# Tiles at multiples of 512 bytes, and a warm-up with fp32r matmuls of ones

## The chip, the cores and the metric

The kernel runs on one core of one Trainium2 chip. The metric is the device time of one execution in microseconds (us); lower is better. The engines are named as in the profile: PE (TensorE, the matmul engine) with PEld for its weight loads, DVE (VectorE), ACT (ScalarE), POOL (GpSimd) and SP (SyncE, which issues most of the transfers). A pair below is two matmuls, one on partitions 0 to 63 and one on partitions 64 to 127, that the array works on side by side.

## What is computed

The reference is a lightweight causal convolution followed by two feed-forward layers without residuals, on 16,384 tokens of width 192:

```python
# x [4, 4096, 192], weight [8, 7]: a softmax over the 7 taps of each of 8 heads,
# then a causal convolution over the sequence with those taps
w = softmax(weight, axis=-1)
out[b, s, h, g] = sum_k w[h, k] * x_pad[b, s + k, h, g]
x = out.reshape(16384, 192)
h = x @ w_in;               x = (h * cos(h)) @ w_out        # layer 1, 192 -> 2048 -> 192
h = max(x @ w_in2, 0);      out = (h * h) @ w_out2          # layer 2, 192 -> 2048 -> 192
```

## The kernel before

Activations lie transposed: features on partitions, tokens along the free dimension, in 32 blocks of T = 512 tokens. The 2048 hidden features are 16 chunks of 128. Every fp32 factor is split into a high and a low part of type fp32r (tiles `xs` for the activations, `g` for the hidden values, `wt1`, `wt2`, `wt3` for the weights), and a product is the sum of three fp32r matmuls (of two in part of the output products).

All matmuls of the two layers have 64 rows: `half` (line 528) takes 64 of the 128 partitions of a weight slice `w[k, o : o + P]` (128 columns) and of a moving tile of 512 columns. `Group.write` issues them alternately for the lower and the upper 64 partitions, so that they run in pairs. `first_products` makes groups for h (input products, line 528 in the profile as `h<-xs,wt`), `second_products` for the output (`o<-g,wt`).

DVE and ACT carry the work between the two products: per chunk of layer 1 a cosine (lines 729, 741, 748, 755) and the split of g (781, 786); per chunk of layer 2 a relu, a square and the same split. They also split the weights: lines 289 to 360, chunk pair by chunk pair, during the first part of the run. DVE makes the convolution of most blocks tap by tap (line 409).

The convolution of the first four blocks (`ON_PE = 4`) is done on PE: six groups of seven pairs of plain fp32 matmuls, with a diagonal matrix of each tap as the weights (`diag`, in the tile `early`) and a shifted block as the moving operand (`x[:, k : k + T]`, line 528 in the profile as `h<-early`). A plain fp32 matmul leaves two MATMUL records in the trace, an fp32r matmul one. ACT (482) and DVE (486) split the results into `xs`.

Ahead of all that stands the warm-up (line 1121): `WARM = 6` pairs of fp32 matmuls of a broadcast constant, `quarter`, into two accumulation banks `o`; nobody reads their result. POOL sets the constants and makes the identity `ident` (lines 174, 175, 446 to 457), from which DVE and ACT make the diagonals once the softmax on DVE (lines 194 to 226) has given `wtap`.

The order of the instructions is planned while the program is built: `Order.run` simulates the engines with fixed costs (`PAIR = 233` ns for a pair) and puts each engine's steps into one fixed order; at run time an engine waits for semaphores in that order. The change leaves these costs alone. Tiles of the pool `const` are laid out in SBUF one behind the other, in the order in which `const.tile` is called.

Of the kernel before, what the change touches and what calls it, by code (L numbers as in the profile page):

```python
# [8 lines left out]
F32 = mybir.dt.float32  # L9
# [9 lines left out]
PAD = K - 1  # L19
DFF = 2048  # L20
NT = B * S
P = 128
R = D - P
T = 512
NB = NT // T
NC = DFF // P
LEAD = 6
WARM = 6
ON_PE = 4
LATE = 4  # L30
EARLY = 4
LAGS = (3, 2)
BUFS = {"raw": 2, "s": 2, "m": 2, "x": 4, "t": 11, "g": 12, "h": 4, "o": 4, "xs": 4}


# [18 lines left out]
def f32(t):  # L54
    return t.bitcast(F32)
# [97 lines left out]
def tile_kernel(  # L153
# [8 lines left out]
    nc = tc.nc  # L162
    V, A, G = nc.vector, nc.scalar, nc.gpsimd
    order = Order()

    const = ctx.enter_context(tc.tile_pool(name="const", bufs=1))
    psum = ctx.enter_context(tc.tile_pool(name="psum", bufs=1, space=PSUM))

    def tiles(kind, shape, dtype, pool=const):
        order.free[kind] = [(0.0, i, pool.tile(shape, dtype, name=f"{kind}{i}")) for i in range(BUFS[kind])]  # L170

# [69 lines left out]
    OA_H, OA_L = (HI + R + P, HI + R + 3 * P), (LO + P, LO + 3 * P)  # L241
    X_H, X_L = HI + R + 4 * P, LO + 4 * P
    OX = (0, HI + U - R)
    wts = [const.tile([P, NC // 2 - n, WC], F32R, name=f"wt{l}") for l, n in ((1, 0), (2, LATE))]

    shared = ctx.enter_context(tc.tile_pool(name="shared", bufs=1))
# [119 lines left out]

    spread_at = {(0, 1): (0, 0, 0), (2, 3): (3, 4, 4)}
    first_slot = {n: at[1 + k] for ab, at in spread_at.items() for k, n in enumerate(ab)}
    tiles("x", [P, T + PAD], F32)
    tiles("t", [P, T], F32)  # L370
    tiles("g", [P, T], F32R)
    tiles("h", [P, T], F32, psum)
    tiles("o", [P, T], F32, psum)
    parts = [[const.tile([P, T], F32R, name=f"xs{i}{j}") for j in range(4)] for i in range(BUFS["xs"])]
    order.free["xs"] = [(0.0, i, p) for i, p in enumerate(parts)]
    def cast(e):
        return A.copy if e == "A" else V.tensor_copy

# [2 lines left out]
    def conv(n, due):  # L381
# [5 lines left out]
        for j in (0, 1):  # L387
# [35 lines left out]
            def high(s, e, y=y, j=j):  # L423
                cast(e)(own.got["xs"][0][2 * j], y.got["t"][0])  # L424
# [15 lines left out]
    for i in range(2 * ON_PE):  # L440
        at = 2 * K * P + i * (T + PAD)
# [2 lines left out]


    G.memset(ident[:, 0], 1.0)
    G.affine_select(
        out=ident[:, 0],
        in_=ident[:, 0],
# [80 lines left out]
    class Item:  # L530
# [15 lines left out]
        def second(self, bank):  # L546
# [3 lines left out]
            acc = self.acc.got["o"][bank]  # L550
            todo = ((OA_L[odd], gh), (OA_H[odd], gh), (OA_H[odd], gl)) if bank == 0 else ((OX[odd], gh), (OX[odd], gl))
            return [(acc, w, o, x) for o, x in todo]
# [112 lines left out]
    def slot(ins):  # L665
# [5 lines left out]
        for k in (0, 1):  # L671
            lag = LAGS[k] if ins or not ending else 0
            if pend[k] and pend[k][0].slot + lag <= s:
                due[k].append(pend[k].pop(0))
                while pend[k] and pend[k][0].slot + LAGS[k] < s:
                    due[k].append(pend[k].pop(0))
# [168 lines left out]
    def ends(it, done):  # L845
# [60 lines left out]
        if l == 0:  # L906
# [11 lines left out]
            def to(j):  # L918
                return own.got["xs"][0][j]

            xh = order.add(
                "xh" + name, high, lambda s, e: cast(e)(to(0), at(ac)), (ac, own), due=due - 3500
            )
            xl = order.add(
# [14 lines left out]
            )  # L939
            yh = order.add(  # L940
                "yh" + name, high, lambda s, e: cast(e)(to(2), at(bc)), (ys, own), due=due - 1500
            )
            yl = order.add(
# [173 lines left out]

    for i in range(WARM):
        for k, rows in enumerate((lower, upper)):
            bank = order.free["o"][k][2]  # L1120
            nc.tensor.matmul(  # L1121
                bank,
                quarter[rows].to_broadcast([R, P]),
                quarter[rows].to_broadcast([R, T]),
                start=i == 0,
                stop=i == WARM - 1,
            )

    with tc.manual_schedule():
        order.run()  # L1130
# [41 lines left out]
```

## Time and profile before

| | |
|---|---|
| time, median of 3 runs | 2333.3 us (2332.58 to 2333.54) |
| profiled execution, span from first to last instruction | 2330.9 us |
| PE busy | 2322.2 us (100% of the span), 19,696 matmul records |
| DVE busy | 1848.8 us (79%) |
| ACT busy | 1936.2 us (83%) |
| POOL busy | 1.4 us |

The profiled execution's span is 2.4 us under the median of the runs: what lies around the first and the last instruction. [...]

### The profile page before, as it was taken

Reading aid. Unit: us, or ns where it says so; the run is one execution under the profiler, and the core shown is the slowest. Engines: PE = TensorE matmul, PEld = TensorE weight load, DVE = VectorE, ACT = ScalarE, POOL = GpSimd, SP = SyncE. Lnnn points to the kernel's source line nnn. Section 1 sums busy time; section 2 is a strip of 40 time slices with the busy share of each in tenths; the row PEclk is TensorE's granted clock in tenths of the full one; section 3 lists DMA queues with packets and bytes.
Section 4 is the critical chain, followed back from the end, with each engine's and each line's share of the span. In section 5 each row is a group of like instructions: output and inputs, shape, how many; then the busy total and the mean of one; then the engine's idle time right before and its main releaser. Section 6 shows DMA issues by size and latency. Waiting matters only on the chain.

```text
span 2330.9 us, 47119 instructions
## 1 busy us (share of the span) xinstructions
PE 2322.2 (100%) x19696; PEld 2262.9 (97%) x19696; DVE 1848.8 (79%) x2963; ACT 1936.2 (83%) x3284; POOL 1.4 (0%) x10
## 2 busy tenths in 40 slices
PE   9999999999999999999999999999999999999998
PEld 5989999999999999999999999999999999999998
DVE  9988988887778887778877788877788877888642
ACT  5888888888888888888888888888888888888886
POOL 0000000000000000000000000000000000000000
PEclk9999999999999999999999999999999999999999
DMA  4120000000000000000000000000000000000000
GB/s 145 42 78 28 6 1 17 17 17 17 1 17 17 17 17 15 3 17 17 17 17 6 13 17 17 17 17 1 17 17 17 17 17 1 17 17 8 8 8 14
DMA packets 30053, 45.17 MB, mean 19 GB/s; under 512 B 3216, under 2 KB 11408, under 8 KB 29840
## 3 DMA queue, kind: packets, MB, share of 16 engines
q1 hardware_dynamic: 29264, 41.10, 5.8%
q8 instruction: 154, 2.52, 0.4%
q10 hardware_dynamic: 576, 1.06, 0.1%
q14 instruction: 59, 0.48, 0.1%
HBM read 29.56 MB, written 12.58 MB: 18 GB/s over the span
## 4 chain that ended last, share of the span: by engine, by line
PE 99%; DVE 0%; ACT 0%; issue 0%; DVEq 0%; POOL 0%; POOLq 0%
PE o L528 51%; PE h L528 47%; PE o L1121 0%; ACT t L765 0%; DVE s L330 0%; DVE g L786 0%; ACT t L774 0%; DVE xs L486 0%; DVE m L307 0%; DVE s L289 0%; DVE m L321 0%; DVE wt L356 0%; ACT s L297 0%; ACT wt L351 0%; DVE t L860 0%
## 5 line engine op out<-in xcount | busy, mean ns | idle before, releaser
L528 PE MATMUL o<-g,wt 64*128 64x512 f32 x10240 | 1432.3, 392 | 1.2 <-DVE g L786 0.4
L528 PE MATMUL h<-xs,wt 64*128 64x512 f32 x9216 | 1312.3, 392 | 0.5
L528 PEld LDWEIGHTS o<-g,wt 64*128 64x128 f32 x10240 | 1186.4, 185 | 25.3 <-PE o L528 5.9
L528 PEld LDWEIGHTS h<-xs,wt 64*128 64x128 f32 x9216 | 1089.0, 185 | 11.9 <-PE h L528 2.9
L786 DVE TENSOR_TENSOR g<-t,g 128x512 fp32r<-128x512 f32 x1024 | 667.4, 686 | 144.4 <-ACT g L781 138.1
L781 ACT CAST g<-t 128x512 fp32r<-128x512 f32 x1024 | 595.5, 617 | 45.7 <-DVE t L755 30.9
L729 ACT ACTIVATE t<-h,quarter 128x512 int32<-128x512 f32 x512 | 350.3, 689 | 203.2 <-PE h L528 197.4
L755 DVE TENSOR_TENSOR t<-t,h 128x512 f32<-128x512 f32 x512 | 348.1, 684 | 168.3 <-ACT t L748 164.4
L741 DVE TENSOR_TENSOR t<-h,t 128x512 f32<-128x512 f32 x512 | 350.8, 689 | 121.1 <-ACT t L729 113.0
L748 ACT ACTIVATE t<-t,right 128x512 f32<-128x512 f32 x512 | 365.1, 718 | 74.2 <-DVE t L741 74.1
L774 ACT ACTIVATE t<-t 128x512 f32<-128x512 f32 x512 | 317.5, 623 | 5.0
L765 ACT ACTIVATE t<-h 128x512 f32<-128x512 f32 x512 | 299.3, 591 | 22.4 <-PE h L528 22.3
L409 DVE SCALAR_TENSOR_TENSOR t<-x,wtap,t 128x512 f32<-128x512 f32 x336 | 250.7, 746 | 3.8
L879 DVE TENSOR_SCALAR t<-o 128x512 f32<-128x512 f32 x60 | 40.8, 680 | 1.4 <-PE o L528 1.4
L428 DVE TENSOR_TENSOR xs<-t,xs 128x512 fp32r<-128x512 f32 x56 | 38.8, 692 | 1.8
L858 ACT ACTIVATE t<-o 128x512 f32<-128x512 f32 x61 | 36.5, 599 | 1.9 <-PE o L528 0.2
L528 PE MATMUL h<-early 64*128 64x512 f32 x168 | 37.7, 594 | 0.2
L528 PEld LDWEIGHTS h<-early 64*128 64x128 f32 x168 | 17.4, 186 | 19.5 <-issue 13.8
L935 DVE TENSOR_TENSOR t<-t,t 128x512 f32<-128x512 f32 x30 | 20.8, 693 | 14.0 <-ACT t L911 13.9
L406 DVE TENSOR_SCALAR t<-x,wtap 128x512 f32<-128x512 f32 x56 | 26.8, 479 | 0.0
L424 DVE CAST xs<-t 128x512 fp32r<-128x512 f32 x56 | 23.3, 416 | 0.0
L946 DVE TENSOR_TENSOR xs<-t,xs 128x512 fp32r<-128x512 f32 x30 | 20.7, 691 | 1.0
(66 smaller groups left out, 285.5 us busy)
## 6 DMA issues: line engine op xcount, KB each, us to landing
x<-in_xp_dram SPq DMA_DIRECT2D x56, 259.0 KB, 3.0
raw<-in_w_dram SPq DMA_DIRECT2D x16, 512.0 KB, 4.0
out_dram<-t SPq DMA_DIRECT2D x32, 256.0 KB, 2.0
out_dram<-t SPq DMA_DIRECT2D x32, 128.0 KB, 2.2
raw<-in_w_dram SPq DMA_DIRECT2D x16, 128.0 KB, 4.2
raw<-in_w_dram SPq DMA_DIRECT2D x32, 64.0 KB, 3.7
early<-in_xp_dram ACTq DMA_DIRECT2D x4, 259.0 KB, 4.8
early<-in_xp_dram SPq DMA_DIRECT2D x4, 259.0 KB, 3.6
```

What stands on the lines that cost most here:

```text
L409: V.scalar_tensor_tensor(out=t, in0=xk, scalar=wk, in1=t, op0=ALU.mult, op1=ALU.add)
L428: V.tensor_tensor(out=lo, in0=y.got["t"][0], in1=f32(h), op=ALU.subtract)
L528: return nc.tensor.matmul(bank, w[k, o : o + P], x[k], start=st, stop=sp)
L729: lambda s, e: A.activation(s.got["t"][0].bitcast(I32), h(), AF.Identity, bias=quarter),
L741: lambda s, e: V.tensor_tensor(out=t(), in0=h(), in1=t().bitcast(I32), op=ALU.subtract),
L748: lambda s, e: A.activation(t(), t(), AF.Sin, scale=2.0 * math.pi, bias=right),
L755: lambda s, e: V.tensor_tensor(out=s.got["t"][0], in0=t(), in1=h(), op=ALU.mult),
L765: lambda s, e: A.activation(s.got["t"][0], h(), AF.Relu),
L774: lambda s, e: A.activation(a.got["t"][0], a.got["t"][0], AF.Square),
L781: "hi" + i, {"A": 620}, lambda s, e: A.copy(s.got["g"][0], d.got["t"][0]), (d,), (("g", 2),), due=late - 1500
L786: lambda s, e: V.tensor_tensor(out=it.hi.got["g"][1], in0=d.got["t"][0], in1=f32(it.hi.got["g"][0]), op=ALU.subtract),
L879: V.tensor_scalar(s.got["t"][0], b(), sc, None, op0=ALU.mult)
```

## The change

It does two things.

First, it moves tiles in SBUF. A tile `gap` of 56 fp32 words (224 bytes) that nobody uses is put ahead of the weights, and the four `x` tiles, whose rows are 2,072 bytes long, are allocated behind `t`, `g` and `xs` instead of ahead of them. The start of each tile in its partition, modulo 512 bytes, in the built programs:

| tiles | before | after |
|---|---|---|
| `wt1`, `wt2` (weights) | 288 | 0 |
| `g`, `xs` (moving operands), `t` | 416 | 0 |
| `raw`, `s`, `m` (weight preparation) | 288 | 0 |
| `early`, later `wt3` (last four chunk pairs of layer 2) | 224 | 448 |
| `x` (convolution inputs) | 288, 320, 352, 384 | 0, 32, 64, 96 |

All slices of the weights begin at multiples of 512 bytes from the start of their tile, and every moving operand of an fp32r matmul begins at the start of its tile. So these operands lie at multiples of 512 after the change, those in `wt3` at 448 modulo 512.

Second, the last three of the six warm-up pairs go. In their place come 43 fp32r matmuls (line 1146 of the new kernel) that multiply a tile of ones, `g0`, by itself: as pairs of 64 rows (`HALVES`) or as single matmuls of 128 rows (`WHOLE`), over 512, 256 or 480 columns, the last from column 8 on. POOL fills that tile with ones, behind the memset of `ident`.

```diff
-WARM = 6
+WARM = 3
+HALVES, WHOLE = (slice(0, R), slice(R, P)), (slice(0, P),)
+RUNS = (
+    (HALVES, 0, T, 5),
+    (WHOLE, 0, T, 7),
+    (HALVES, 0, T, 2),
+    (WHOLE, 0, T, 4),
+    (HALVES, 0, T, 2),
+    (WHOLE, 0, T // 2, 6),
+    (HALVES, 8, 480, 4),
+)
+GAP = 56
...
+    const.tile([P, GAP], F32, name="gap")
     wts = [const.tile([P, NC // 2 - n, WC], F32R, name=f"wt{l}") for l, n in ((1, 0), (2, LATE))]
...
-    tiles("x", [P, T + PAD], F32)
     tiles("t", [P, T], F32)
...
     order.free["xs"] = [(0.0, i, p) for i, p in enumerate(parts)]
+    tiles("x", [P, T + PAD], F32)
...
     G.memset(ident[:, 0], 1.0)
+    ones = order.free["g"][0][2]
+    G.memset(f32(ones), 1.0)
...
+    for spans, at, n, times in RUNS:
+        for i in range(times):
+            for k, rows in enumerate(spans):
+                bank = order.free["o"][k][2]
+                nc.tensor.matmul(
+                    bank[:, 0:n], ones[rows, 0:P], ones[rows, at : at + n], start=i == 0, stop=i == times - 1
+                )
```

PE before, the end of the warm-up and the first products of the convolution (`early` holds the diagonals and the shifted blocks; the brackets name the engines and queues that an instruction waits for):

```order
L1121 MATMUL o_111<-quarter 128x512
L1121 MATMUL o_112<-quarter 128x512
L528 MATMUL h_107<-early 128x512 [waits DMAHW0_49,DVE_49]
L528 MATMUL h_108<-early 128x512 [waits DMAHW4_49,Activation_49]
L528 MATMUL h_107<-early 128x512 [waits Activation_49]
```

PE now, first where the fp32 pairs of the warm-up give way to the matmuls of ones (`g_92` is the tile of ones):

```order
L1135 MATMUL o_108<-quarter 128x512
L1135 MATMUL o_109<-quarter 128x512
L1146 MATMUL o_108<-g_92 128x512 [waits Pool_49]
L1146 MATMUL o_109<-g_92 128x512
L1146 MATMUL o_108<-g_92 128x512
L1146 MATMUL o_109<-g_92 128x512
```

and at the end of the warm-up, where the same convolution products follow:

```order
L1146 MATMUL o_108<-g_92 128x256 x6
L1146 MATMUL o_108<-g_92 128x480
L1146 MATMUL o_109<-g_92 128x480
L1146 MATMUL o_108<-g_92 128x480
L1146 MATMUL o_109<-g_92 128x480
L1146 MATMUL o_108<-g_92 128x480
L1146 MATMUL o_109<-g_92 128x480
L1146 MATMUL o_108<-g_92 128x480
L1146 MATMUL o_109<-g_92 128x480
L542 MATMUL h_104<-early 128x512 [waits DMAHW0_49,DVE_49]
L542 MATMUL h_105<-early 128x512 [waits DMAHW4_49,Activation_49]
```

Six fp32 matmuls have gone and 43 fp32r matmuls stand in their place, the first of them with a wait for POOL. Behind them PE's instructions stand in the order they had.

POOL before, from its first constants on:

```order
L174 MEMSET quarter 128x1
L175 MEMSET right 128x1
L446 MEMSET ident 128x128
L447 ISA
L447 AFFINE_SELECT ident<-ident 128x128
L457 TENSOR_TENSOR ident<-ident 128x64 x2
```

POOL now, at the same place:

```order
L185 MEMSET quarter 128x1
L186 MEMSET right 128x1
L458 MEMSET ident 128x128
L460 MEMSET g_92 128x512
L461 ISA
L461 AFFINE_SELECT ident<-ident 128x128 [waits Pool_49]
L471 TENSOR_TENSOR ident<-ident 128x64 [waits Pool_49]
```

One memset of 512 columns has come ahead of the making of the identity. On DVE, ACT and SP no instruction is added, removed or moved.

## Rows read from the trace of the kernel before

**Rows 1.** The page: span, busy time by engine, granted PE clock, chain that ended last.

```profile
span 2330.9 us, 47119 instructions
...
PE 2322.2 (100%) x19696; PEld 2262.9 (97%) x19696; DVE 1848.8 (79%) x2963; ACT 1936.2 (83%) x3284; POOL 1.4 (0%) x10
...
PEclk9999999999999999999999999999999999999999
...
PE 99%; DVE 0%; ACT 0%; issue 0%; DVEq 0%; POOL 0%; POOLq 0%
```

**Rows 2.** PE by line and shape: count | busy us, mean ns of a record.

```profile
L528 PE MATMUL o<-g,wt 64*128 64x512 f32 x10240 | 1432.3, 392 | 1.2 <-DVE g L786 0.4
L528 PE MATMUL h<-xs,wt 64*128 64x512 f32 x9216 | 1312.3, 392 | 0.5
...
L528 PE MATMUL o<-quarter 64*128 64x256 f32 x16 | 1.9, 376 | 0.0
```

**Rows 3.** Timeline of PE mid-run: start us, us from first start to last end, count.

```profile
1001.51 1.39 PE L528 MATMUL o<-g,wt 64*128 64x512 f32 x10
1002.68 0.91 PE L528 MATMUL h<-xs,wt 64*128 64x512 f32 x6
1003.38 1.38 PE L528 MATMUL o<-g,wt 64*128 64x512 f32 x10
1004.53 1.62 PE L528 MATMUL h<-xs,wt 64*128 64x512 f32 x12
...
1007.78 1.38 PE L528 MATMUL o<-g,wt 64*128 64x512 f32 x10
```

**Rows 4.** Timeline of PE from 2300 us on.

```profile
2312.05 1.46 PE L528 MATMUL o<-g,wt 64*128 64x512 f32 x10
...
2316.49 8.45 PE L528 MATMUL o<-g,wt 64*128 64x512 f32 x70
```

**Rows 5.** Stretches: busy us (count) of PE, PEld, DVE, ACT, POOL; then granted clock.

```profile
600.00:1000.00 400.00, 400.00 (x3442) 397.27 (x3441) 318.47 (x505) 337.77 (x573) 0.00 (x0) 1.00 0.04 14
...
2306.00:2322.00 16.00, 16.00 (x141) 15.80 (x139) 5.17 (x8) 10.11 (x20) 0.00 (x0) 1.00 0.00 1
```

**Rows 6.** Timeline of PE in the first 45 us.

```profile
7.74 19.09 PE L528 MATMUL h<-early 64*128 64x512 f32 x84
26.26 5.67 PE L528 MATMUL h<-xs,wt 64*128 64x512 f32 x36
31.77 1.90 PE L528 MATMUL o<-quarter 64*128 64x256 f32 x16
```

**Rows 7.** Timeline of PEld, the warm-up: a pair of records each.

```profile
4.59 0.19 PEld L1121 LDWEIGHTS o<-quarter 64*128 64x128 f32 x2 [0.24 <-issue]
5.02 0.19 PEld L1121 LDWEIGHTS o<-quarter 64*128 64x128 f32 x2 [0.24 <-issue]
...
7.74 1.25 PEld L528 LDWEIGHTS h<-early 64*128 64x128 f32 x8 [0.81 <-DVE early L469]
```

**Rows 8.** Timeline of PEld in the convolution products.

```profile
21.08 0.19 PEld L528 LDWEIGHTS h<-early 64*128 64x128 f32 x2 [0.24 <-issue]
21.52 0.19 PEld L528 LDWEIGHTS h<-early 64*128 64x128 f32 x2 [0.24 <-issue]
```

**Rows 9.** Timeline of PE behind a wait: one pair alone, then two pairs.

```profile
33.74 0.50 PE L528 MATMUL h<-xs,wt 64*128 64x512 f32 x2
...
33.74 0.73 PE L528 MATMUL h<-xs,wt 64*128 64x512 f32 x4
```

**Rows 10.** Timelines of POOL, ACT and DVE near the start.

```profile
0.86 0.20 POOL L446 MEMSET ident<- 128x128 f32 x1
...
15.34 0.59 ACT L482 CAST xs<-h 128x512 fp32r<-128x512 f32 x1 [1.07 <-PE h L528]
...
15.44 0.95 DVE L330 SCALAR_TENSOR_TENSOR s<-raw,s 128x768 int32<-128x768 int32 x1
16.31 0.68 DVE L486 TENSOR_TENSOR xs<-h,xs 128x512 fp32r<-128x512 f32 x1
```

**Rows 11.** The chain that ended last, first 60 us: start us, us, what.

```profile
7.76 6.37 PE h L528 x28
...
53.31 0.59 ACT xs L482
...
54.66 0.04 DVE wt L356
```

## Prediction

> **What bounds the kernel now.** [...] The pace comes from starts in the timeline, not from record lengths, which overlap. From 1003.38 to 1007.78 us PE starts 10 + 12 + 10 + 6 = 38 matmuls, of which the last two rows have the same sizes as the two ahead of them [rows 3]: 19 pairs in 4.40 us, 232 ns a pair. There are (10,240 + 9,216) / 2 = 9,728 such pairs [rows 2], 2257 us or 97% of the span. The rest is the warm-up, the convolution on PE and short waits. One nanosecond on a pair is thus worth 9.7 us; one microsecond at the start is worth one microsecond, if it is not taken back.
>
> A measurement of this kernel can tell about 0.2%, 4.7 us, from no change: "same" below means 2328.6 to 2338.0 us.
>
> **The change, part by part: the tiles.** The order on DVE, ACT and SP is untouched, and PE's is untouched behind the warm-up, so nothing of the 97% changes except the addresses. The question is whether 232 ns contains a price for operands at 416 (moving) and 288 or 224 (weights) modulo 512. There is something to explain. A pair of fp32 matmul records of 256 columns takes (1.90 - 0.376) / 7 = 0.218 us [rows 2, 6], and a pair of fp32 records of 512 columns 0.43 us, twice that [rows 8]. An fp32r pair of 512 columns needs 14 ns more than the first. Three readings:
>
> - Other engines disturb PE's reads. No: near the end, with DVE busy for 5.2 of 16 us instead of 318 of 400 [rows 5], 38 matmuls take 4.44 us from 2312.05 to 2316.49 [rows 4] (the rows between repeat the pattern of rows 3), 234 ns a pair.
> - The addresses cost it. Against that stand the convolution products: their blocks start at steps of 4 bytes, one per tap, their weights at 224 modulo 512, and yet each pair of records comes 0.43 us behind the last, the same as the warm-up's with its broadcast constant [rows 7, 8]. So at the fp32 pace no address costs anything. It could still cost at the fp32r pace, which takes columns almost twice as fast; no row has an fp32r matmul at another address.
> - It belongs to the fp32r form at any address. Nothing speaks against this.
>
> I take zero for the tiles, since the only rows with many different addresses show no difference; the bounds are zero and 14 ns a pair. For a loss I see no row: before, all moving operands already had one common remainder modulo 512.
>
> [...]
>
> **The warm-up.** Its last three pairs leave six pairs of records of 0.43 us, the first at 5.02 us [rows 7]; they end near 7.6, and the convolution starts at 7.74, when the first diagonal is there. PE executes in order, so the matmuls of ones start at 5.02 and the convolution waits for them. Their length:
>
> - 9 pairs of halves of 512 columns: 9 x 0.232 = 2.09 us.
> - 4 pairs of 480 columns: 4 x 0.232 x 480 / 512 = 0.87 us.
> - 11 whole matmuls of 512 columns. No row has one. Bounds: 0.218 us, the fastest pair of records over as many array cycles (2.40 in all), and 0.73 - 0.39 = 0.34 us, the step from a first pair to a second behind a wait [rows 9], if none of them overlaps with its neighbour (3.74). I take 0.232, since a pair of halves occupies the whole array just as one whole matmul does: 2.55 us.
> - 6 whole ones of 256 columns: half of that, 0.116 us, 0.70 in all; bounds 0.65 and 6 x (0.116 + 0.108) = 1.34, with the same 0.108 us (0.34 - 0.232) on each.
>
> The sum is 6.21 us, bounds 6.01 and 8.04. The warm-up ends at 11.23 us (11.03 to 13.06), and the convolution starts 3.5 us later (3.3 to 5.3).
>
> The wait for POOL costs nothing: the memset of 128 columns is a 0.20 us record at 0.86 [rows 10], four times as many columns are an estimated 0.8 us, and PE asks for the ones at 5.02. Their delay to the identity is hidden too: the diagonals are needed only at 11.2 now.
>
> How much is taken back? Almost nothing. The convolution's 84 records run without a break to 26.26, where the first layer follows at once [rows 6]. DVE works in order too, and its first instruction that needs PE, line 486 at 16.31, follows line 330 without a pause [rows 10]; its operand is there at 15.34 + 0.59 = 15.93, so it has 0.38 us to spare. Where the chain leaves PE for ACT and DVE at 53.31 [rows 11], DVE's queue decides, and DVE is late by the delay less that 0.38. Net: 3.1 us (2.9 to 5.3; the upper end without the 0.38). Later waits hang on semaphores of these same engines, none on a fixed time, so they move along.
>
> Against the profiled execution: 2330.9 + 3.1 = 2334.0 span. The 2.4 us between span and median stay: 2333.3 + 3.1 = **2336.4 us**, 0.13% more.
>
> **The rivals.**
>
> 1. The addresses did cost the 14 ns (faster). For it: the excess exists, it is independent of the other engines, and the fp32r pace is the one that asks most of the reads. Against it: the convolution products. Time: 2336.4 - 9,728 x 0.0144 = 2196 us; ACT's busy share would go from 84% [rows 5] to 90%, which may give some waits back, so 2196 to 2215. Part of the 14 ns gives anything between; from 0.8 ns a pair on it would count as faster.
> [...]
>
> 2. The whole matmuls don't overlap (slower). They follow one another into one accumulation bank with all 128 rows, where before two halves alternated. If each of the 17 pays 0.34 or 0.224 us, the warm-up ends at 13.06 and the kernel takes 2338.2 to 2338.6. It decides from a warm-up sum of about 7.8 us, that is from some 0.33 us for a whole matmul of 512 columns. For it: fresh starts do cost 0.108 us [rows 9]. Against it: a sequence without waits has shown no such step anywhere. Taking whole record lengths, 0.39 and 0.376 us, gives 9.5 us for the sum and 2340.
>
> 3. The change doesn't do all it says: the last four chunk pairs of layer 2 lie at 448. This would cut rival 1 by a quarter of layer 2's pairs, an eighth of all, to about 2214; it changes nothing for the forecast.
>
> **How the numbers follow.** Forecast, no effect of the addresses and a later start: 0.64. Rivals 1 and 3 in full or in part: 0.19. Rival 2, or another loss at the start or from the new addresses: 0.17. The forecast's own range is 2335.8 to 2338, with 1 us for the spread of the runs 2334.8 to 2338. The range reaches up to 2342 (rival 2 with whole records, and the spread of runs) and down to 2328, a gain of about 1 ns a pair; the larger gains, under 0.2, are left out. Faster 0.19, same 0.64, slower 0.17.
>
> **What would show it.** Right: mid-run, 38 matmuls still take 4.40 us; the first convolution product starts near 11.2 us; line 486 starts about 3.1 us later than 16.31; the whole matmuls of ones come every 0.23 us. Rival 1 shows as fewer than 4.3 us for 38 matmuls, and already in the ones: their first pairs of halves, at 0 modulo 512, would be closer together per column than the pairs from column 8 on. Rival 2 shows as steps of 0.3 us or more between whole matmuls. The prediction is wrong if the pace mid-run differs by 0.5 ns a pair, or if the delay at 7.74 us is not found again at 26 us.

## The result

The changed kernel takes 2293.98 us (median of 4 runs, 2293.3 to 2294.37) beside 2333.42 us for the kernel before on the same chip, 0.9831 times the time, 95% interval 0.9817 to 0.9844. It is 39 us faster, where 3 us slower was forecast and a gain of up to some 5 us was allowed for.

The page of the changed kernel (parts 1, 2 and 4) answers to [rows 1]:

```profile
span 2291.6 us, 47182 instructions
...
PE 2282.5 (100%) x19727; PEld 1988.1 (87%) x19727; DVE 1842.1 (80%) x2963; ACT 1934.0 (84%) x3284; POOL 1.8 (0%) x11
...
PEclk9999999999999999999999999999999999999999
...
PE 99%; DVE 1%; ACT 0%; issue 0%; DVEq 0%; POOL 0%; POOLq 0%
```

PE still holds the chain, at the same granted clock, and the counts on DVE and ACT are the same. What moved is the pace. In stretches of 800 us mid-run (columns: busy us and count of PE, PEld, DVE, ACT, POOL; then clock, DMA share, GB/s), the kernel before and the changed one:

```profile
1400.00:2200.00 800.00, 800.00 (x6882) 794.61 (x6880) 641.80 (x1017) 676.32 (x1146) 0.00 (x0) 1.00 0.04 14
```

```profile
1400.00:2200.00 800.00, 800.00 (x7024) 704.70 (x7022) 643.83 (x1023) 687.80 (x1166) 0.00 (x0) 1.00 0.05 14
```

Some three records of each count only reach over the edge. So 800 / (6879 / 2) = 232.6 ns a pair before, and 800 / (7021 / 2) = 227.9 now. 4.7 ns on 9,728 pairs is 46 us; the span fell by 39.3.

Most of the missing 7 us is at the start. The weight loads of the changed kernel's warm-up show it (start us, us, count; the matmuls start with them or at most one step later):

```profile
4.81 0.19 PEld L1146 LDWEIGHTS o<-g 64*128 64x128 f32 x2 [0.24 <-issue]
5.24 0.89 PEld L1146 LDWEIGHTS o<-g 64*128 64x128 f32 x8 [0.24 <-issue]
6.49 1.46 PEld L1146 LDWEIGHTS o<-g 128*128 128x128 f32 x7 [0.36 <-issue]
8.30 0.30 PEld L1146 LDWEIGHTS o<-g 64*128 64x128 f32 x4 [0.35 <-issue]
8.96 0.76 PEld L1146 LDWEIGHTS o<-g 128*128 128x128 f32 x4 [0.36 <-issue]
10.09 0.30 PEld L1146 LDWEIGHTS o<-g 64*128 64x128 f32 x4 [0.36 <-issue]
10.75 1.64 PEld L1146 LDWEIGHTS o<-g 128*128 128x128 f32 x14 [0.36 <-issue]
```

The seven whole matmuls last from 6.49 to 8.30, the next two pairs to 8.96, the four whole ones to 10.09: 1.81, 0.66 and 1.13 us, each 0.2 us more than 0.23 us a piece (a pair counted as one piece). The convolution follows at 12.63 us (timeline of PE), 4.9 us later than in [rows 6]:

```profile
4.84 7.96 PE L1146 MATMUL o<-g 64*128 64x512 f32 x43
12.63 18.92 PE L542 MATMUL h<-early 64*128 64x512 f32 x84
30.99 5.49 PE L542 MATMUL h<-xs,wt 64*128 64x512 f32 x36
```

### The profile page after: what moved, and what is told of

Same layout as the page of the kernel before. It is cut to its first block, busy times and chain, and to the rows that moved or that the text cites. A ratio compares the mean times of both kernels' runs of the same rounds, so it can differ in the third digit from the quotient of the medians.

```text
span 2291.6 us, 47182 instructions
## 1 busy us (share of the span) xinstructions
PE 2282.5 (100%) x19727; PEld 1988.1 (87%) x19727; DVE 1842.1 (80%) x2963; ACT 1934.0 (84%) x3284; POOL 1.8 (0%) x11
## 4 chain that ended last, share of the span: by engine, by line
PE 99%; DVE 1%; ACT 0%; issue 0%; DVEq 0%; POOL 0%; POOLq 0%
PE o L542 51%; PE h L542 47%; PE o L1146 0%; PE o L1135 0%; ACT t L779 0%; DVE s L342 0%; DVE g L800 0%; ACT t L788 0%; DVE t L769 0%; DVE xs L500 0%; DVE m L319 0%; DVE s L301 0%; DVE m L333 0%; DVE wt L368 0%; ACT s L309 0%
## 5 line engine op out<-in xcount | busy, mean ns | idle before, releaser
L542 PE MATMUL o<-g,wt 64*128 64x512 f32 x10240 | 1362.7, 388 | 1.3 <-DVE g L800 0.5
L542 PE MATMUL h<-xs,wt 64*128 64x512 f32 x9216 | 1244.6, 388 | 0.5
L542 PEld LDWEIGHTS o<-g,wt 64*128 64x128 f32 x10240 | 1035.8, 184 | 142.9 <-PE o L542 5.9
L542 PEld LDWEIGHTS h<-xs,wt 64*128 64x128 f32 x9216 | 935.5, 184 | 128.2 <-PE h L542 2.9
```

The source lines that it names most:

```text
L542: return nc.tensor.matmul(bank, w[k, o : o + P], x[k], start=st, stop=sp)
```

## The experiments

"Difference" below is the remainder modulo 256 of (start of the moving operand minus start of the weights in their partition), in bytes.

### The two halves of the change, each alone

The new addresses without the new warm-up (`e1_align_only`):

```diff
-WARM = 3
+WARM = 6
...
-    ones = order.free["g"][0][2]
-    G.memset(f32(ones), 1.0)
...
-    for spans, at, n, times in RUNS:
-        ...
```

> The new addresses alone, with the old warm-up of six fp32 pairs. In the trace of the changed kernel the first convolution product starts at 12.63 us instead of 7.74, 4.9 us later, of which DVE takes back 0.38. If the addresses give the whole gain and the warm-up only costs: 2294.0 - 4.5 = 2289.5 us (2288 to 2291), mid-run pace 228 ns a pair. If the matmuls of ones had part in the gain: above 2294. If the pace came from something other than addresses: 2333.

Measured: 2289.17 us, 0.9811 (0.9797 to 0.9826). The first branch: the addresses give all the gain, 43.9 us of it.

The new warm-up with the old addresses (`e8_runs_only`), as an edit against the changed kernel:

```diff
-    const.tile([P, GAP], F32, name="gap")
...
+    tiles("x", [P, T + PAD], F32)
     tiles("t", [P, T], F32)
...
-    tiles("x", [P, T + PAD], F32)
```

> The old addresses with the new warm-up (three fp32 pairs, then the 43 matmuls of ones). In the trace of the changed kernel the convolution starts 4.9 us later; less the 0.38 us that DVE has to spare: 2333.1 + 4.5 = 2337.6 us (2336.5 to 2338.5). If PE's delay were taken back later by waits: 2333 to 2335.

Measured: 2338.04 us beside 2333.07, 1.0021 (1.0011 to 1.003): 5.0 us lost, as expected. The two halves add up: 4.8 us lie between the changed kernel and e1. Little of the delay comes back: in the traces the changed kernel is 4.80 us behind e1 at the first convolution product, 4.46 us behind some 45 us later and 4.70 us at the last matmul.

How late the convolution starts also differs between executions. In the profiled one of e8 it starts at 13.76 us, 6.0 us later than before, and the weight loads of the warm-up still come 0.85 us apart beyond 5 us, where in the kernel before they come 0.43 us apart from 4.16 us on:

```profile
3.68 0.34 PEld L1133 LDWEIGHTS o<-quarter 64*128 64x128 f32 x2 [0.51 <-issue]
4.53 0.34 PEld L1133 LDWEIGHTS o<-quarter 64*128 64x128 f32 x2 [0.51 <-issue]
5.38 0.34 PEld L1144 LDWEIGHTS o<-g 64*128 64x128 f32 x2 [0.51 <-issue]
```

The first clock record of the trace, 1.00, stands at 6.50 us in e8, at 3.77 us in the kernel before and at 4.22 us in the changed kernel. A slice of the page is some 58 us long and doesn't show that. So a start that is read from one profile can be a microsecond off, here 6.0 us later beside 4.9.

### Which operand

Moving operands at 0, weights left at 288 (`e2_moving_only`: no `gap` ahead of the weights, the same 224 bytes ahead of `t`), and weights at 0 with the moving operands at 32 (`e3_weights_only`: one `x` tile back ahead of `t`). Edits against e1:

```diff
-    const.tile([P, GAP], F32, name="gap")
...
+    const.tile([P, GAP], F32, name="gap")
     tiles("t", [P, T], F32)
```

```diff
+    x0 = const.tile([P, T + PAD], F32, name="x0")
     tiles("t", [P, T], F32)
...
-    tiles("x", [P, T + PAD], F32)
+    order.free["x"] = [(0.0, 0, x0)] + [(0.0, i, const.tile([P, T + PAD], F32, name=f"x{i}")) for i in (1, 2, 3)]
```

> Old warm-up; moving operands at 0 modulo 512, weights wt1 and wt2 left at 288 (wt3 at 448). Theory M (the moving operand's address costs the 4 to 5 ns a pair): about 2290 us and 228 ns a pair, as with both. Theory W (the weights' address costs it): about 2333 us and 232 ns in layer 1. Theory B (each has its share): in between, 2300 to 2322.

> Old warm-up; weights wt1 and wt2 at 0 modulo 512, wt3 at 448, moving operands at 32 (before 416, both 32 modulo 64). Theory W: about 2290 us, 228 ns a pair. Theory M: about 2333 us, 232 ns. Theory B: 2300 to 2322, and the savings of this kernel and of moving-only add up to those of both, 44 us.

Measured: 2330.74 us (0.9991, 0.9981 to 1.0) and 2339.78 us (1.0028, 1.0017 to 1.004). No theory foresaw this: aligning the moving operands alone gives 2.4 us and aligning the weights alone nothing, where both together give 43.9; aligned weights beside operands 32 bytes off even make the kernel 6.7 us slower than before. In the same stretch of 800 us, e2, then e3:

```profile
1400.00:2200.00 800.00, 800.00 (x6888) 783.65 (x6886) 642.39 (x1019) 676.64 (x1147) 0.00 (x0) 1.00 0.04 14
```

```profile
1400.00:2200.00 800.00, 800.00 (x6861) 794.87 (x6859) 640.39 (x1015) 673.36 (x1141) 0.00 (x0) 1.00 0.04 13
```

By the same working 232.4 and 233.3 ns a pair.

### The last tile

In the change `wt3` lies at 448, 64 bytes short of a multiple of 512. `e4_align_all` brings it to 0, with a filler and with the identity built in a tile of the weight preparation:

```diff
     tiles("x", [P, T + PAD], F32)
+    const.tile([P, 144], F32, name="gap3")
...
-    ident = const.tile([P, 2, P], F32, name="ident")
+    ident = f32(order.free["m"][1][2][:, 0 : 2 * P]).rearrange("p (j c) -> p j c", j=2)
```

> Old warm-up; all of the changed kernel's addresses, and wt3 (last four chunk pairs of layer 2) at 0 instead of 448; the identity is built in a tile of the weight preparation to make room. In the changed kernel matmuls on wt3 follow one another at 229 ns on average instead of 227.5 on wt1 and wt2. If 64 bytes short of a multiple of 512 costs the weights 1.5 ns: 9728 / 4 / 2... a quarter of layer 2's and so an eighth to a quarter of all pairs, 1200 to 2400 x 1.5 ns = 2 to 4 us under the align-only kernel, 2286 to 2288. If the difference is chance: the same as align-only within 1 us.

Measured: 2277.66 us, 0.9763 (0.9748 to 0.9777), 11.5 us under e1, where 2 to 4 were expected. This version beats both kernels. Its stretch:

```profile
1400.00:2200.00 800.00, 800.00 (x7060) 685.03 (x7058) 638.86 (x1015) 690.54 (x1171) 0.00 (x0) 1.00 0.04 13
```

800 / (7057 / 2) = 226.7 ns. The expectation had the share of `wt3` wrong. It holds four of layer 2's eight chunk pairs, so half of that layer's matmuls and a quarter of all. And mid-run nearly every pair is one matmul of layer 1 and one of layer 2 (`first_products` and `second_products` take one item of each list), so one on `wt3` stands in half of all pairs. With the program's order of matmuls laid over the starts of e1's trace (300 to 2250 us), pairs of `wt1` and `wt2` come 227.1 ns apart on average and pairs of `wt1` and `wt3` 228.8; in e4 it is 226.7 and 226.8. 2.0 ns on half of the 9,728 pairs and 0.4 on the other half make 11.7 us.

### Alignment, or the same remainder

The align-all kernel with all tiles behind the gap moved by 32 and by 64 bytes (`e5_shift32`, `e6_shift64`: `GAP = 64` and `GAP = 72`), and with 256 bytes between weights and moving operands (`e10_diff256`: a filler of 64 words ahead of `t`).

> The align-all kernel (2277.7 us) with everything behind the gap moved by 32 bytes: weights, wt3 and moving operands all at 32 modulo 512. The moving-only kernel (0 and 288) and the weights-only kernel (32 and 0) gained nothing, so two theories are left. Theory R (what counts is that weights and moving operands have the same remainder): 2277.7 us, 226.8 ns a pair, as unshifted. Theory A (both must lie at a multiple of some power of two by themselves): 2330 to 2340 us, 232 ns or more.

> The same with 64 bytes: all at 64 modulo 512. Theory R: 2277.7 us. Theory A with 64 as the power of two: 2277.7 us too. Theory A with 128 or more: slower; wt3 at 448 (64 modulo 128) with moving operands at 0 takes 229.2 ns in the align-only kernel, so 2300 us or above.

> The align-all kernel (2277.7 us) with the moving operands at 256 modulo 512, weights and wt3 at 0. Theory P: the difference counts modulo 256, so 2278 us and 226.8 ns a pair. If the period is 512: about 2330 us.

Measured: 2278.34 (0.9766, 0.9752 to 0.9781), 2278.79 (0.9768, 0.9754 to 0.9783) and 2279.7 us (0.9771, 0.9754 to 0.9787). Theory A falls: the multiple of 512 is not what counts. Theory R stands, with one addition from e10: remainders that differ by 256 count as the same (227.0 ns a pair mid-run, by the working above, beside 226.7). With everything at 32, where nothing lies at a multiple of 64, the pace is the same:

```profile
1400.00:2200.00 800.00, 800.00 (x7058) 670.71 (x7056) 639.10 (x1014) 690.27 (x1170) 0.00 (x0) 1.00 0.04 13
```

### The pace at each difference

Two kernels put runs of 24 pairs of ones at chosen addresses in place of the change's 43 matmuls (`e7_probe`, `e9_probe2`; the ones lie in `wt2`, and the diff shows e7's loop). Their times, 2394.78 and 2433.63 us of one run each, hold the longer warm-up and are not of interest.

```diff
+    for spans, w_at, m_at in PROBE:
+        w, m = 1024 + w_at // 4, m_at // 4
+        for n, times in ((T, TIMES), (T // 2, 1)):
+            for i in range(times):
+                for k, rows in enumerate(spans):
+                    bank = order.free["o"][k][2]
+                    nc.tensor.matmul(
+                        bank[:, 0:n], ones[rows, w : w + P], ones[rows, m : m + n], start=i == 0, stop=i == times - 1
+                    )
```

> The changed kernel, with its 43 matmuls of ones replaced by 19 runs of 24 fp32r matmul pairs of 512 columns each (the last two runs: single matmuls of 128 rows), weights and moving operand at chosen remainders modulo 512, a matmul of 256 columns behind each run as a mark. The warm-up gets about 100 us longer; the pace within a run is what is read. Theory R: 227 ns where both remainders agree, (0, 0), (32, 32), (64, 64), and 230 to 235 elsewhere. Theory A: 227 ns only where both are multiples of 64 or 128. If the pace of ones in one place doesn't depend on the address, the loss needs the changing weights and operands of the real products.

> Runs of 24 fp32r pairs of ones as in the first probe, read by the pace within a run. First 20 runs: weights at 0, moving operand at every 16 bytes from 0 to 240, then at 4, 8, 252 and 0. Theory P (the pace depends on moving minus weights modulo 256, as the first probe's 19 runs suggest): 226.7 ns at 0, 229 at 64, 233 at 32, 128, 192 and 224, and values between or above at the steps that have no row yet; whether any difference beats 226.7 is open. Last 6 runs: weights or moving operand replaced by a broadcast of one word. Theory C (the weight load's reads and the moving operand's reads meet in SBUF): with the weights broadcast the pace no longer depends on the address, about 218 to 227 at 0, 32 and 128; the same with the moving operand broadcast. If only one of the two matters, the other broadcast leaves 233 at 32.

Timeline of PE in windows inside single runs of the second probe, weights at 0, moving operand at 0, 64 and 128, then with the weights a broadcast of one word and the moving operand at 32, then with the weights at 0 and the moving operand a broadcast (start us, us from first start to last end, count):

```profile
5.94 4.47 PE L1149 MATMUL o<-wt 64*128 64x512 f32 x38
...
28.84 4.51 PE L1149 MATMUL o<-wt 64*128 64x512 f32 x38
...
51.52 4.60 PE L1149 MATMUL o<-wt 64*128 64x512 f32 x38
...
125.65 4.57 PE L1149 MATMUL o<-wt 64*128 64x512 f32 x38
...
137.17 4.32 PE L1149 MATMUL o<-wt 64*128 64x512 f32 x38
```

Less a last record of 0.39 us, over 18 steps: 227, 229, 234, 232 and 218 ns. The same from the starts of all pairs of a run but the first five, in ns:

| difference | second probe, weights at 0 | first probe, (weights, moving) |
|---|---|---|
| 0 | 226.7, again 228.1 | (0, 0) 226.6, twice; (0, 256) 226.7; (256, 0) 227.8; (32, 32) 227.3; (64, 64) 226.7 |
| 4, 8, 16 | 236.7, 233.3, 232.0 | |
| 32, 48 | 233.2, 233.3 | (0, 32) 233.4 |
| 64 | 228.9 | (0, 64) 228.9; (448, 0) 228.9 |
| 80, 96, 112 | 231.1, 233.3, 231.1 | |
| 128 | 233.3 | (288, 416) 232.8; (0, 128) 232.7; (128, 0) 232.7 |
| 144, 160, 176 | 233.2, 234.4, 233.3 | (0, 416) 234.4 |
| 192 | 233.3 | (64, 0) 233.3; (224, 416) 233.3 |
| 208, 224, 240 | 234.8, 233.3, 233.3 | (32, 0) 233.3; (288, 0) 233.3 |
| 252 | 226.7 | |
| moving operand a broadcast (weights at 0, at 32, a broadcast too) | 218.7 to 218.9 | |
| weights a broadcast | 231.1 to 231.8 at 0, 32 and 128 | |

Cases of the same difference agree within 1.5 ns, wherever they lie, and whole matmuls of 128 rows go like pairs of halves: 227.0 at (0, 0), 232.5 at (288, 416). Theory P holds in all of them. Theory C is half borne out: with the weights a broadcast the pace no longer depends on the address, as it said, but at 231 to 232 ns and not at the 218 to 227 it named. The table gives the mid-run pace of the kernels within 0.6 ns. `wt1` and `wt2` serve three quarters of the matmuls, `wt3` one quarter; no probe had pairs whose two halves differ, so that the mean of the two stands for them is an assumption, and for the changed kernel it comes out too low:

| kernel | differences, wt1 and wt2; wt3 | by the table | mid-run |
|---|---|---|---|
| before | 128; 192 | 0.75 x 232.8 + 0.25 x 233.3 = 232.9 | 232.6 |
| changed | 0; 64 | 0.75 x 226.7 + 0.25 x 228.9 = 227.3 | 227.9 |
| moving only | 224; 64 | 232.2 | 232.4 |
| weights only | 32; 96 | 233.2 | 233.3 |
| align all | 0; 0 | 226.7 | 226.7 |

### What lies behind it

Theory C, that the weight load's reads and the moving operand's meet, was tried further with shorter weight loads and fewer moving columns (`e12_probe3`, 2380.61 us, the same loop with weights of 128, 64 and 32 columns and 512, 384 and 256 moving columns).

> 20 runs of 24 fp32r pairs of ones: weights of 128, 64 and 32 columns with 512 moving columns, then 128 weight columns with 384 and 256 moving columns; in each the moving operand at 0, 32 and 128 bytes from the weights' remainder, and as a broadcast of one word (218.7 ns with 128 and 512 columns in the second probe). Theory C (the reads of the weight load and those of the moving operand meet): the excess over the broadcast, 8 ns at 0 and 14.5 ns at 32 and 128 bytes, shrinks with the weight columns, to about half and a quarter (4 and 2 ns, 7 and 4 ns), and stays the same in ns with fewer moving columns. Theory S (the moving operand's reads are slower by themselves): the excess doesn't depend on the weight columns, and shrinks with the moving columns, to three quarters and half. A constant excess in both would mean a price per matmul that neither explains.

Pace from the starts of the pairs (all but the first seven), in ns:

| weight columns, moving columns | at 0 | at 32 | at 128 | broadcast |
|---|---|---|---|---|
| 128, 512 | 226.6 | 233.3 | 232.3 | 218.7 |
| 64, 512 | 229.7 | 230.8 | 229.1 | 218.7 |
| 32, 512 | 231.7 | 232.2 | 230.2 | 218.7 |
| 128, 384 | 173.4 | 173.3 | 175.8 | 165.4 |
| 128, 256 | 120.0 | 117.6 | 118.8 | 112.0 |

Neither theory holds. Shorter weight loads don't shrink the excess over the broadcast (theory C): it is 10 to 14 ns with 64 and with 32 columns, at each difference. With fewer moving columns it shrinks at 32 and 128, from 14.6 and 13.6 ns to 5.6 and 6.8, as theory S says, but not at 0, where it is 8 ns with 512, 384 and 256 columns. And theory S has no place for the weights' address, and at 128 and 512 that address decides between 7.9 and 14.6 ns in this run. So: a moving operand that walks through SBUF costs 6 to 18 ns a pair over one that stands still (117.6 over 112.0 ns in e12, 236.7 over 218.7 in e9), and with full weights and 512 columns the difference of the two addresses sets how much (226.6 ns at 0, 233.3 at 32). Why, stays open.

### The planner's cost

`e11_plan227` is the align-all kernel with `PAIR` at 227 in the planner.

> The align-all kernel with the planner's cost of a pair at 227 ns instead of 233, so that its order fits the new pace. Mid-run PE never waits, so only the first 300 us can change, where PE loses some 9 us to waits: 2275 to 2281 us. A loss or a gain of over 4 us would show that the order was bound to the old pace.

Measured: 2279.69 us (0.9771, 0.9757 to 0.9786), 2.0 us over align-all and inside the expected range. Planning with the new pace gains nothing; the order was not bound to the old one.

## Why the prediction was wrong

**What bounds the kernel: right.** PE bounds it [rows 1], and one nanosecond a pair is worth 9.7 us: from before to align-all the pace fell by 5.9 ns, 57 us by that rule, and the time by 55.5.

**The tiles taken at zero: the step that failed.** It rested on the convolution products, whose many addresses all gave 0.43 us [rows 8]. Those are plain fp32 records, where a pair of 512 columns takes 0.43 us and not the 0.232 of an fp32r pair, and at that pace the warm-up's broadcast takes 0.43 us too [rows 7]. The prediction itself noted that no row had an fp32r matmul at another address, and still took the one row with many addresses as the nearest. The term measured 4.6 ns a pair in the change (e1) and 5.9 with all tiles, inside its bounds of zero and 14. The prediction's own sign of being wrong, 0.5 ns a pair mid-run, is met: the changed kernel's pace differs by 4.7.

**The list of readings: incomplete.** "The addresses" was read as each operand's own alignment. The relation of two operands was not among the three readings, and "all moving operands already had one common remainder" looked at the wrong pair: the common remainder that counts is the one with the weights (226.6 to 228.1 ns a pair where it is the same, 231 to 237 at 16 differences, e7 and e9). The third reading, the fp32r form at any address, is wrong as well: the row of 0.218 us [rows 2, 6] has a broadcast of one word as its moving operand, and fp32r pairs with such an operand take 218.7 ns (e9). The 14 ns, 232 less 218, set a moving operand that walks through SBUF against one that stands still.

**The quiet end: read wrongly.** That 38 matmuls take 4.44 us near the end [rows 4] did exclude the other engines. But those pairs are not like the ones mid-run: by the program's order all of them use `wt3` alone, at a difference of 192, for which the probes give 233.3 ns. With `wt3` at 0 the same rows of e4 lie 4.30 us apart, 226 ns a pair:

```profile
2257.59 1.30 PE L531 MATMUL o<-g,wt 64*128 64x512 f32 x10
...
2261.89 6.31 PE L531 MATMUL o<-g,wt 64*128 64x512 f32 x54
```

**The warm-up: right in kind, too small.** Whole matmuls do follow at about 0.23 us, and rival 2 didn't occur. But the ones begin at 5.24 us and not at 5.02, and the sum of 6.21 us left out the 0.2 us at each change between halves and whole (0.66 us over two steps of the changed kernel in place of 0.46), some 1.2 us in all; the ones last from 5.24 to 12.63, 7.4 us. With the old addresses that costs 5.0 us (e8) and not 3.1. The lower bound of 0.218 us was set by array cycles, which no run shows; an fp32r pair of 512 columns took 0.219 us with a broadcast as the moving operand, and 0.227 or more with one that walks (e9). DVE's line 486, now 500, starts 4.37 us later than in [rows 10], behind a convolution that starts 4.9 us later, so about 0.5 us is taken back there. Over the run it is 0.34 us at most (4.80 less 4.46 against e1), near the forecast 0.38:

```profile
15.52 0.95 DVE L342 SCALAR_TENSOR_TENSOR s<-raw,s 128x768 int32<-128x768 int32 x1
20.68 0.69 DVE L500 TENSOR_TENSOR xs<-h,xs 128x512 fp32r<-128x512 f32 x1 [4.21 <-ACT xs L496]
```

**POOL: right.** The memset of ones is a record of 0.53 us at 1.00, long done when PE asks:

```profile
1.00 0.53 POOL L460 MEMSET g<- 128x512 f32 x1
```

**The rivals.** What came is rival 1 in part: the fp32r form's 14 ns over the fastest pair hold about 6 that go with the addresses and about 8 that no address removed, and that a broadcast moving operand does. Its early sign failed: in the changed kernel's trace the first pairs of ones, at difference 0, come 0.225 to 0.236 us apart from the second on, and those from column 8 on, behind a first step of 0.32, 0.215 and 0.223 us apart, 0.229 and 0.238 for 512 columns. These few steps could not tell: the first run of e7, at difference 0 too, takes 245 ns a pair over all its steps and 226.6 without the first five. Rival 3 named the right tile but half its share: `wt3` has half of layer 2's matmuls, not a quarter, and kept 11.5 us back.

## What to carry to other kernels

Where PE is the bound and its pace is some per cent over the fastest row of the same form, ask of every operand's address, and of the operands' addresses relative to each other: change one, the other, and both by the same amount. A row at half the pace need not show what costs time at the full pace: here the fp32 pairs of the convolution came 0.43 us apart at starts 4 bytes from each other, and fp32r pairs 226.6 to 236.7 ns at the differences tried. Nor is a row with a broadcast operand a measure for operands that walk (218.7 ns beside 226.6 and more). And work that was put ahead of the first useful instruction of the bounding engine cost nearly all of the delay it made: 4.80 us at the first convolution product, 4.70 at the last matmul.

## What the runs showed that was not expected

- fp32r matmuls with 128 weight columns and 512 moving columns take 226.6 to 228.1 ns a pair where weights and moving operand start at the same remainder modulo 256 bytes, 228.9 ns with the moving operand 64 bytes on, and 231 to 237 at 16 other differences tried; 4 bytes below (252) gave 226.7 as well, 4 bytes above 236.7.
- The same with the moving operand a broadcast of one word: 218.7 to 218.9 ns, with the weights at 0, at 32 or a broadcast too.
- PE's step from a pair of 64-row matmuls to a single one of 128 rows, or back, costs about 0.2 us over the first two steps (0.32 and 0.34 us in place of 0.23 in the changed kernel). A new run of like pairs costs nothing of the kind (in e7 some 0.345 us from the last pair of 512 columns, over the mark of 256, to the next run).
